# Where a decode layer's input x is loaded, and who copies its key tiles, in a kernel fed by one long stream of weights

## The chip, the cores and the metric

One core of a Trainium2 chip runs one launch. The metric is the device time in microseconds (us), here the median of three runs.

## The reference

One token goes through a transformer layer whose attention and gated feed-forward stand side by side on the same normalised input. All is float32.

```python
x  = A_x                                  # (1, 1, 1024)
xn = layernorm(x)                         # eps 1e-5, no weights
# attention: 32 query heads, 4 key heads, 128 wide; the last 4096 of 65536 cached positions
q = (xn @ wq)                             # wq 1024 x 4096
p = softmax(q k^T * 128**-0.5);  o = p v  # k, v: 4 x 4096 x 128
a = o @ wo                                # wo 4096 x 1024
# feed-forward
h = gelu(xn @ w_gate) * (xn @ w_up)       # 1024 x 3584 each
b = h @ w_down                            # 3584 x 1024
return x + a + b
```

Nearly all of the work is to read these weights and the window of the caches once: 94.38 MB by the profile.

## The kernel before

All large tensors pass through one tile in SBUF, `ring`, of 128 partitions x 32768 columns (16.8 MB). The list `PLAN` says in which order the loads are issued, to which column of the ring each goes, and which earlier load's data must have been used up before it may be issued. In order: `q` 0 and 1 (the halves of wq), `k` 0, `v` 0, `g` 0 (half of w_gate), `k` 1, `v` 1, `g` 1, `ua` 0, `ub` 0, `u` 1 (w_up), `o` 0 and 1 (wo), `m`, and `d` 0 to 2 (w_down). Every one of them is issued on SyncE's queue by `load`, so SyncE's queue is the order of the stream; a load that has to wait for its part of the ring holds up those behind it. The entry `m` stands for `load_moved`: ten small loads (`moved`) of a part of w_down's last rows.

A recording layer (`Flow`) stands between the code and the engines. Each operation goes to its engine in the order in which the code calls it. From the places that operations read and write it works out which must wait for which, and gives each waiting instruction its semaphores. All operations thus carry one line, L225, in the profile.

The first transfers do not go through the ring. `x_rows`, x as 2 rows of 512, is what the layer norm reads. `x_out`, x spread over four of the 128 partitions, is added to the output at the very end (`downs`, the addition of `out_p` and `x_out`). Both are issued on ScalarE's queue at the program's start: two transfers for `x_rows`, one for each row, and two for `x_out`. GpSimd builds the identity matrix `ident` at the start, and VectorE fills and builds the other constants. `layer_norm` then transposes `x_rows` on TensorE (`xt_p`, in the tag `tp`) and leaves the normalised x in `xz`. `xz` is what every product with wq, w_gate and w_up needs. Such a product is split: even rows go to TensorE (`blocks`, tile `acc`), odd rows are scaled and summed on VectorE (`add_scaled`, tile `part`).

Each load of keys holds two of the four key heads. For each head `transpose_keys` makes eight tiles `kT`: TensorE transposes four 128x128 blocks into one of two PSUM buffers (tag `tp`), and then one engine copies that buffer to SBUF. The argument `vector` lists the tiles that VectorE copies; ScalarE copies the others. Because there are two buffers, TensorE's tile i+2 waits for the copy of tile i. `scores` multiplies the eight tiles by the queries and finds the maximum on VectorE (`reduce_max`, an addition of `away`, a second `reduce_max`, and `bias`); `exponentials` runs on ScalarE. For a pair of heads the code stands in this order:

```python
transpose_keys(2 * i, kn[:, :half], range(8), (1, 4, 6))
if i == 0:
    queries(q_sb)
s = scores(2 * i)
transpose_keys(2 * i + 1, kn[:, half:], range(4), ())
exponentials(2 * i, s)
transpose_keys(2 * i + 1, kn[:, half:], range(4, 8), (4, 5, 7))
s = scores(2 * i + 1)
```

When the second head's last transposition is done, the keys' part of the ring is free and the next load into it (`k` 1, later `ua` 0) may be issued.

Of the kernel before, what the change touches and what calls it, by code (L numbers as in the profile page):

```python
# [19 lines left out]
NJ = D // (NR * P)  # L20
# [13 lines left out]
ROW = (31, 32, 95, 96)  # L34
# [231 lines left out]
def decode_layer(nc, x, k_cache, v_cache, wq, wo, w_gate, w_up, w_down, out):  # L266
# [16 lines left out]
    def source(kind, i):  # L283
        if kind == "q":
            return fours(wq, i)
        if kind == "g":
            return fours(w_gate, i)
        if kind[0] == "u":
            return fours(w_up, i)[:, {"u": slice(NR), "ua": slice(2), "ub": slice(2, NR)}[kind]]
        if kind in "kv":  # L290
            cache = k_cache if kind == "k" else v_cache
            return windows(cache, i)
        if kind == "o":
            return grouped(wo, P * WIDE * i, WIDE)
        return grouped(w_down, P * sum(DOWN[:i]), DOWN[i])
# [4 lines left out]
    def load(key, at):  # L300
        kind, i = key
        if kind == "m":
            load_moved()
            return
        src = source(*key)
        if kind in "kv":

            loaded[key] = dst = ring[:, at:at + RING // 4]
            if kind == "v":
                nc.sync.dma_start(dst, src)  # L310
            else:
                for odd in range(2):
                    nc.sync.dma_start(dst[odd:P:2], src[:, odd])
            return
        rows, n = src.shape[1:]
        loaded[key] = ring[:, at:at + rows * n]
        dst = loaded[key].rearrange("p (t n) -> p t n", n=n)
        pieces = PIECES[i] if kind == "d" else (0, rows)
        if key == ("d", 2):
            end = 2 * n - MC  # L320
            nc.gpsimd.memset(loaded[key][:, end:2 * n], 0.0)
            both = src[:, 0:2].rearrange("p t n -> p (t n)")
            nc.sync.dma_start(loaded[key][0:P:2, :2 * n], both[0:P:2])
            nc.sync.dma_start(loaded[key][1:P:4, :2 * n], both[1:P:4])
            nc.sync.dma_start(loaded[key][3:P:4, :end], both[3:P:4, :end])
            pieces = pieces[1:]
        for t, end in zip(pieces, pieces[1:]):
            ends = (0, n // 2, 3 * n // 4, n) if key == ("d", 2) and end == rows else (0, n)
            for cols in (slice(*cut) for cut in zip(ends, ends[1:])):
                nc.sync.dma_start(dst[:, t:end, cols], src[:, t:end, cols])  # L330
# [4 lines left out]
    def load_moved():  # L335


        rest = w_down[DF - 4 * P:, D - MC:].rearrange("(r x) n -> x r n", x=16)[13]
        for s, a, first, count, step in MOVED:
            for j in range(step):  # L340
                to = 32 * a + j
                nc.sync.dma_start(
                    moved[to:to + 4 * (count // step):4, s], rest[first + j:first + count:step]
                )

    def used(key):

        for new, at, old in PLAN:
            if old == key:
                load(new, at)  # L350


    x_rows = work.tile([NJ, NR * P], F32, name="x_rows")
    x_in = x.rearrange("a b (j p) -> (a b j) p", j=NJ)
    for j in range(NJ):
        nc.scalar.dma_start(x_rows[j:j + 1, :], x_in[j:j + 1, :])
    x_out = work.tile([P, CO], F32, name="x_out")
    nc.vector.memset(x_out, 0.0)
    x_in = x.rearrange("a b (h c n) -> (a b c) h n", h=2, c=4)
    for c in (0, 2):  # L360
        nc.scalar.dma_start(
            x_out[ROW[c]:ROW[c] + 2, :].rearrange("c (h n) -> c h n", h=2), x_in[c:c + 2]
        )

    ident = consts.tile([P, P], F32, name="ident")
    nc.gpsimd.memset(ident, 0.0)
# [43 lines left out]
    def small(name):  # L410
        return psum.tile([P, NB], F32, name=name, tag="tp", bufs=2)
# [56 lines left out]
    def project(kind, jj, w, rows, count):  # L468
        n = count * NB
        for k, r in enumerate(rows):  # L470
            first = jj == 0 and r < 2
            if first and r == 0:
                acc[kind] = psum.tile([P, 2, NB], F32, name="acc_" + kind, tag="acc")
                part[kind] = work.tile([P, 8 * NB], F32, name="part", tag="part")
            wr = w[:, k * n:(k + 1) * n]
            if r % 2 == 0:
                blocks(kind, xz[:, r, jj, :], wr, count, first, False)
            else:
                add_scaled(part[kind][:, :n], wr, xz[:, r, jj, 0:1], first)

    def projected(kind, count):
        blocks(kind, unit, part[kind], count, False, True)

    def query_rows():
        q_sb = work.tile([P, 2, NB], F32, name="q_sb", tag="rows")
        nc.scalar.activation(q_sb, acc["q"], AF.Copy)
        return q_sb

    def queries(q_sb):
        q_p = psum.tile([P, 2, 4, 4], F32, name="q_p", tag="tp", bufs=2)  # L490
        for b in range(2):
            for hh in range(4):
                nc.tensor.matmul(
                    q_p[:, b, hh, :], q_sb[:, b, hh * P:(hh + 1) * P], ident[:, 0:P:32],
                    start=True, stop=True,
                )
            nc.vector.tensor_copy(
                qz[:, b, 0:16].rearrange("p (s t h) -> p s t h", s=2, t=2),
                q_p[:, b].rearrange("p h (s t) -> p s t h", s=2),
            )  # L500
# [10 lines left out]
    def transpose_keys(g, kn, steps, vector):  # L511
        if g not in keys:
            keys[g] = work.tile([P, 8, NB], F32, name="kT")
        for i in steps:
            t_p = small("kt_p")
            for jj in range(4):
                j = 4 * i + jj
                nc.tensor.transpose(t_p[:, jj * P:(jj + 1) * P], kn[:, j * DH:(j + 1) * DH], ident)
            if i in vector:
                nc.vector.tensor_copy(keys[g][:, i, :], t_p)  # L520
            else:
                nc.scalar.activation(keys[g][:, i, :], t_p, AF.Copy)
# [19 lines left out]
    def exponentials(g, s):  # L542
        p = work.tile([P, 2, NB], F32, name="p", bufs=2)
        for odd in range(2):
            nc.scalar.activation(
                p.rearrange("p b (n odd) -> p odd (b n)", odd=2)[:, odd], s[:, odd], AF.Exp,
                bias=bias[:, g, odd:odd + 1], scale=SCALE, accum_out=l[:, g, odd:odd + 1],
            )
        probs[g] = p
# [223 lines left out]
    half = RING // 8  # L773
    for key, _, _ in PLAN:
        kind, i = key
        if kind == "m":
            continue
        if kind == "q":
            project("q", i, loaded.pop(key), range(NR), 8)
        elif kind == "k":  # L780
            kn = loaded.pop(key)
            if i == 0:
                projected("q", 8)
                q_sb = query_rows()
            transpose_keys(2 * i, kn[:, :half], range(8), (1, 4, 6))
            if i == 0:
                queries(q_sb)

            s = scores(2 * i)
            transpose_keys(2 * i + 1, kn[:, half:], range(4), ())  # L790
            exponentials(2 * i, s)
            transpose_keys(2 * i + 1, kn[:, half:], range(4, 8), (4, 5, 7))
            s = scores(2 * i + 1)
        elif kind == "v":
            vn = loaded.pop(key)
            pT = transpose_probs(2 * i)
            exponentials(2 * i + 1, s)
            values(2 * i, pT, vn[:, :half])
            values(2 * i + 1, transpose_probs(2 * i + 1), vn[:, half:])
            if i == 1:  # L800
                maxima()
        elif kind == "g":
            project("g", i, loaded.pop(key), range(NR), NA)
            if i == 1:
                state = factors()
                projected("g", NA)
                gelu()
        elif kind in ("ua", "ub", "u"):
            taken = {"ua": (0, 1), "ub": (2, 3), "u": range(NR)}[kind]
            project("u", i, loaded.pop(key), taken, NA)  # L810
            if kind == "ua":
                normalizers(*state)
            elif kind == "ub":
                heads()
        elif kind == "o":
            if i == 0:
                projected("u", NA)
                gated()
            outputs(i)
            if i == 0:  # L820
                hidden()
        elif i == 2:
            downs()
        used(key)
# [26 lines left out]
```

## Time and profile before

| what | value |
|---|---|
| median of 3 runs (lowest, highest) | 226.16 us (226.12, 226.31) |
| the profiled execution | 226.15 us |
| its span, from first to last instruction | 224.8 us |
| TensorE, VectorE, ScalarE, GpSimd busy | 126.0, 112.1, 28.2, 2.8 us |
| read from HBM | 94.38 MB, 420 GB/s over the span |
| time of SyncE's queue's packets (q1), of 16 DMA engines' span | 97.8% |

The span is 1.35 us shorter than the execution's time. q1 is SyncE's queue, q10 ScalarE's; q8 and q14 fetch instructions and the like. Where a row gives start and length, both are microseconds, the start from the span's start.

### The profile page before, as it was taken

What the parts mean: (1) busy time and instruction counts of PE and PEld (TensorE: products, weight loads), DVE (VectorE), ACT (ScalarE), POOL (GpSimd) and SP (SyncE); (2) the same over time, 40 slices, a digit from 0 to 9 for tenths busy, and PEclk for the clock granted to TensorE, in tenths of its full rate; (3) what the DMA queues carried; (4) which work ended last, traced back from release to release, by engine and by line L of the source; (5) the groups of instructions that cost most, each with busy time, mean ns of one, the idle gap of its engine ahead of it and who ended that gap; (6) DMA issues with size and microseconds to landing.
All of it is one profiled execution on the core that took longest, in us unless ns stands there. A gap on an engine that the chain in (4) does not pass through costs nothing.

```text
span 224.8 us, 2511 instructions
## 1 busy us (share of the span) xinstructions
PE 126.0 (56%) x1107; PEld 65.6 (29%) x1107; DVE 112.1 (50%) x142; ACT 28.2 (13%) x54; POOL 2.8 (1%) x9
## 2 busy tenths in 40 slices
PE   0120910539899891999836751237308988900976
PEld 0010200104634731755601110001003887400442
DVE  7030920591333282336039489339708932992942
ACT  2030000002415600454400220000000000000000
POOL 3000000000000000000000000000000000010000
PEclk9999975596969999799988795557965855665699
DMA  9889889799997999999989999999989989999994
GB/s 374 374 385 548 373 373 560 338 408 464 439 490 338 429 443 452 391 488 408 472 355 449 434 449 429 490 399 420 469 385 455 467 385 461 434 397 394 426 407 172
DMA packets 3194, 94.53 MB, mean 421 GB/s; under 512 B 446, under 2 KB 718, under 8 KB 1040
## 3 DMA queue, kind: packets, MB, share of 16 engines
q1 hardware_dynamic: 3160, 94.38, 97.8%
q8 instruction: 8, 0.13, 0.2%
q14 instruction: 2, 0.02, 0.0%
q10 hardware_dynamic: 24, 0.01, 0.0%
HBM read 94.38 MB, written 0.00 MB: 420 GB/s over the span
## 4 chain that ended last, share of the span: by engine, by line
DMA 67%; DVE 20%; PE 10%; SPq 1%; ACT 1%; issue 1%; POOL 0%; DVEq 0%
DMA ring<-in_B_w_gate 26%; DMA ring<-in_A_wq 18%; DMA ring<-in_A_wo 13%; DVE part L225 13%; DMA ring<-in_B_w_down 10%; PE tp L225 6%; PE out L225 3%; DVE out_part L225 3%; DVE rows L225 2%; SPq L225 1%; PE acc L225 1%; DVE g_sb L225 1%; ACT kT L225 1%; DVE hz L225 1%; DVE kT L225 0%
## 5 line engine op out<-in xcount | busy, mean ns | idle before, releaser
L225 PE MATMUL acc<-ring,xz 128*32 128x512 f32 x176 | 32.2, 808 | 37.3 <-DMA ring<-in_A_wq 22.2
L225 DVE SCALAR_TENSOR_TENSOR part<-ring,xz,part 128x3584 f32<-128x3584 f32 (+1 forms) x9 | 37.2, 4129 | 22.0 <-DMA ring<-in_A_wq 12.5
L225 PE MATMUL tp<-ident,ring 128*128 128x128 f32 x128 | 21.0, 309 | 7.1 <-DMA ring<-in_A_k_cache 5.0
L225 PEld LDWEIGHTS acc<-ring,xz 128*32 128x32 f32 x176 | 7.2, 139 | 58.2 <-issue 26.7
L225 DVE SCALAR_TENSOR_TENSOR out_part<-ring,oz,out_part 128x1024 f32<-128x1024 f32 x16 | 20.6, 1285 | 0.6
L225 PEld LDWEIGHTS tp<-ident,ring 128*128 128x128 f32 x128 | 15.4, 154 | 16.7 <-DMA ring<-in_A_k_cache 5.9
L225 PE MATMUL out<-ring,hz 128*32 128x256 f32 x168 | 12.1, 438 | 13.5 <-DMA ring<-in_B_w_down 13.4
L225 DVE COPY kT<-tp 128x512 f32<-128x512 f32 x12 | 8.1, 690 | 19.1 <-PE tp L225 19.1
L225 PE MATMUL out<-ring,oz 128*32 128x256 f32 x120 | 12.0, 586 | 9.6 <-DMA ring<-in_A_wo 9.6
L225 ACT ACTIVATE kT<-tp 128x512 f32<-128x512 f32 x20 | 11.5, 596 | 26.6 <-PE tp L225 26.6
L225 PE MATMUL tp<-ident,kT 128*128 128x4 f32 (+4 forms) x64 | 13.4, 343 | 1.6 <-DVE hz L225 1.6
L225 PEld LDWEIGHTS tp<-ident,kT 128*128 128x128 f32 (+2 forms) x64 | 13.1, 294 | 2.2 <-DVE hz L225 1.8
L225 PE MATMUL acc<-part,units 128*32 128x512 f32 x44 | 8.1, 817 | 8.7 <-DVE part L225 8.7
L225 DVE TENSOR_SCALAR part<-ring,xz 128x3584 f32<-128x3584 f32 (+1 forms) x3 | 6.5, 2171 | 12.3 <-DMA ring<-in_A_wq 7.5
L225 PEld LDWEIGHTS out<-ring,hz 128*32 128x32 f32 x168 | 5.6, 125 | 20.0 <-DMA ring<-in_B_w_down 15.8
L225 PEld LDWEIGHTS out<-ring,oz 128*32 128x32 f32 x120 | 5.7, 166 | 16.0 <-DMA ring<-in_A_wo 10.6
L225 DVE SCALAR_TENSOR_TENSOR out_part<-ring,hz,out_part 128x1024 f32<-128x1024 f32 x6 | 7.7, 1285 | 4.9 <-DMA ring<-in_B_w_down 4.7
L225 PE MATMUL s<-kT,qz 128*32 128x512 f32 x64 | 9.3, 709 | 0.0
L225 DVE TENSOR_REDUCE m<-s 128x2 f32<-128x1024 f32 x4 | 4.9, 1225 | 7.7 <-PE s L225 7.7
L225 PE MATMUL o<-ring,pT 128*32 128x128 f32 x256 | 7.8, 274 | 1.0 <-ACT pT L225 1.0
L225 PEld LDWEIGHTS o<-ring,pT 128*32 128x32 f32 x256 | 6.7, 110 | 1.9 <-ACT pT L225 1.9
L225 PE MATMUL tp<-ident,x_rows 2*128 2x2 f32 x4 | 0.6, 253 | 10.4 <-DMA x_rows<-in_A_x 10.4
(96 smaller groups left out, 73.3 us busy)
## 6 DMA issues: line engine op xcount, KB each, us to landing
ring<-in_B_w_gate SPq DMA_DIRECT2D x2, 7168.0 KB, 29.5
ring<-in_A_k_cache SPq DMA_DIRECT2D x4, 2048.0 KB, 19.0
ring<-in_A_v_cache SPq DMA_DIRECT2D x2, 4096.0 KB, 26.1
ring<-in_B_w_up SPq DMA_DIRECT2D x2, 3584.0 KB, 22.3
ring<-in_B_w_up SPq DMA_DIRECT2D x1, 7168.0 KB, 25.8
ring<-in_B_w_down SPq DMA_DIRECT2D x2, 2048.0 KB, 20.7
ring<-in_B_w_down SPq DMA_DIRECT2D x2, 512.0 KB, 21.1
ring<-in_B_w_down SPq DMA_DIRECT2D x2, 256.0 KB, 21.2
```

What stands on the lines that cost most here:

```text
L225: return lambda *a, **k: self.flow.issue(self.engine, lambda: call(*a, **k))
```

## The change

Three edits. The two transfers for `x_rows` become one of 2x512, issued on GpSimd's queue, ahead of all that GpSimd does for `ident`. The two transfers for `x_out` move from ScalarE's queue at the start to SyncE's queue, behind the ten loads of `moved` and ahead of `d` 0. And the tiles 1 and 3 of each pair's second head are copied by VectorE and no longer by ScalarE.

```diff
         if kind == "m":
             load_moved()
+            load_out()
             return
...
     x_rows = work.tile([NJ, NR * P], F32, name="x_rows")
-    x_in = x.rearrange("a b (j p) -> (a b j) p", j=NJ)
-    for j in range(NJ):
-        nc.scalar.dma_start(x_rows[j:j + 1, :], x_in[j:j + 1, :])
+    nc.gpsimd.dma_start(x_rows, x.rearrange("a b (j p) -> (a b j) p", j=NJ))
     x_out = work.tile([P, CO], F32, name="x_out")
     nc.vector.memset(x_out, 0.0)
-    x_in = x.rearrange("a b (h c n) -> (a b c) h n", h=2, c=4)
-    for c in (0, 2):
-        nc.scalar.dma_start(
-            x_out[ROW[c]:ROW[c] + 2, :].rearrange("c (h n) -> c h n", h=2), x_in[c:c + 2]
-        )
+
+    def load_out():
+        x_in = x.rearrange("a b (h c n) -> (a b c) h n", h=2, c=4)
+        for c in (0, 2):
+            nc.sync.dma_start(
+                x_out[ROW[c]:ROW[c] + 2, :].rearrange("c (h n) -> c h n", h=2), x_in[c:c + 2]
+            )
...
-            transpose_keys(2 * i + 1, kn[:, half:], range(4), ())
+            transpose_keys(2 * i + 1, kn[:, half:], range(4), (1, 3))
```

ScalarE's queue at the program's start (`x_rows` and `x_out` are the two loads of x, `st` and `zero` belong to the layer norm), with what the change takes out:

```order
-L225 DMA x_rows<-in_A_x 1x512 x2
-L225 DMA x_out<-in_A_x 2x2x128 x2
 L225 ACT_TABLE_LOAD
 L225 ACTIVATE st<-st 128x1
```

All four of its first transfers are gone, and its first instruction is now the table load.

SyncE's queue behind the second half of wo (`moved` are the small loads, `ring` the weights, here `d` 0 and the two halves of `d` 1):

```order
 L225 DMA moved<-in_B_w_down 5x768
 L225 DMA moved<-in_B_w_down 3x768
+L225 DMA x_out<-in_A_x 2x2x128 x2
 L225 DMA ring<-in_B_w_down 128x16384
 L225 DMA ring<-in_B_w_down 128x4096 x2
```

Two issues more stand ahead of the first load of w_down.

VectorE in the first pair of heads (`m` and `bias` are the end of `scores` of the pair's first head, `kT` the copies for its second head, the second `m_0` its scores):

```order
 L225 TENSOR_REDUCE m<-m_0 128x1
 L225 SCALAR_TENSOR_TENSOR bias<-m,away 128x2
-L225 COPY kT<-tp 128x512 x3
+L225 COPY kT<-tp 128x512 x5
 L225 TENSOR_REDUCE m_0<-s 128x2
 L225 TENSOR_TENSOR m_0<-m_0,away 128x2
```

The two added copies stand behind the first head's maximum and `bias`, not beside them; the same happens in the second pair. TensorE's order is unchanged.

## The prediction

> **What bounds the kernel now.** I read the page's head and queues first, then the stretches by window, then the chain that ended last.
>
> ```profile
> span 224.8 us, 2511 instructions
> DMA  9889889799997999999989999999989989999994
> ...
> q1 hardware_dynamic: 3160, 94.38, 97.8%
> q8 instruction: 8, 0.13, 0.2%
> ...
> q10 hardware_dynamic: 24, 0.01, 0.0%
> ```
>
> The sixteen DMA engines are busy in nearly every slice, and SyncE's queue (q1) alone fills 97.8% of their span. The windows (length, then busy time of TensorE, its weight loads, VectorE, ScalarE, GpSimd, then clock, DMA share and GB/s) say the same of each stage:
>
> ```profile
> 2.00:42.00 40.00, 8.11 (x44) 3.23 (x48) 12.30 (x31) 2.97 (x4) 0.65 (x2) 0.87 0.95 411
> 42.00:80.00 38.00, 31.92 (x307) 17.19 (x310) 17.18 (x19) 11.84 (x23) 0.00 (x0) 0.87 1.01 434
> 80.00:116.00 36.00, 24.46 (x270) 14.98 (x264) 13.81 (x20) 10.81 (x22) 0.00 (x0) 0.95 1.00 428
> 116.00:169.00 53.00, 22.83 (x117) 5.33 (x117) 33.76 (x30) 2.54 (x5) 0.00 (x0) 0.70 1.01 437
> 169.00:220.00 51.00, 35.66 (x336) 23.86 (x336) 32.86 (x36) 0.00 (x0) 0.74 (x1) 0.64 0.98 422
> ```
>
> No compute engine fills its window; DMA does, in all five. The chain's pieces (start, length, what) show why:
>
> ```profile
> 0.73 0.42 SPq L225
> ...
> 1.21 40.66 DMA ring<-in_A_wq
> ...
> 51.00 28.54 DMA ring<-in_B_w_gate
> ...
> 200.11 21.38 DMA ring<-in_B_w_down
> ```
>
> A load issued at 51.00 lands at 79.54 because its bytes stand behind others. So an engine that finishes later costs nothing until it makes SyncE issue a load so late that the stream runs dry. The time is the stream's start, 94.38 MB at its rate, and a tail of some 3 us after the last landing at 221.49. I cost each edit against that.
>
> **x_rows on GpSimd.** The timeline of the start (start, length, engine, operation):
>
> ```profile
> 0.73 0.79 ACTq L225 DMA_DIRECT2D x_rows<-in_A_x  x2
> 0.73 0.20 POOL L225 MEMSET ident<- 128x128 f32 x1 [0.29 <-POOLq L839]
> 0.73 0.89 SPq L225 DMA_DIRECT2D ring<-in_A_wq  x2
> ...
> 1.56 0.57 ACTq L225 DMA_DIRECT2D x_out<-in_A_x  x2
> ...
> 5.34 0.22 DVE L225 TENSOR_SCALAR away<-away 128x1 f32<-128x1 f32 x2
> ...
> 10.36 0.61 PE L225 MATMUL tp<-ident,x_rows 2*128 2x2 f32 x4 [10.36 <-DMA x_rows<-in_A_x]
> ...
> 14.94 0.23 DVE L225 TENSOR_SCALAR xz<-xc,st 128x8 f32<-128x8 f32 x1
> ...
> 22.67 6.25 PE L225 MATMUL acc<-ring,xz 128*32 128x512 f32 x32 [9.16 <-DMA ring<-in_A_wq]
> ...
> 26.43 1.17 SPq L225 DMA_DIRECT2D ring<-in_A_k_cache  x2
> 29.53 0.57 SPq L225 DMA_DIRECT2D ring<-in_A_v_cache  x1
> ```
>
> x was issued at 0.73 and let TensorE start at 10.36, 9.6 us later, since it shares the DMA engines with wq. From there `xz` takes 15.17 - 10.36 = 4.8 us, and the product with wq's first half cannot start before its load is in at 22.67. So x may be 22.67 - 15.17 = 7.5 us late before anything moves. Beyond that, only the next load counts: `k` 0 is issued 26.43 - 22.67 = 3.8 us after that product's start, and must be in the queue before wq's second half lands at 41.87, less the 0.5 us that the first load took from issue to its first data (0.73 to 1.21). So x may land as late as 41.87 - 0.5 - 3.8 - 4.8 = 32.8 us, against 10.4 now.
>
> When will it land? The trace has no transfer from GpSimd. The early end is about now, at 8 to 11 us: I assume that one transfer waits once behind wq's packets where two wait twice, but starts somewhat later. For the late end I let GpSimd get nothing done until VectorE has finished its constants (5.34 + 0.22 = 5.6 us) and then give x the 21.4 us of the last w_down load, the nearest row of a short load behind a full queue: 27 us. Even that is below 32.8. I take 12 us, nearer to the row of the same data, and a cost of 0. GpSimd's transfer also stands ahead of `ident`; `ident` is needed by VectorE's constants and by x's own transposition, and GpSimd could give it up to 9 us late before TensorE misses it.
>
> The Trainium skill speaks against this edit: its page "SBUF — State Buffer", section "SBUF: two separate sides", says that a transfer issued from GpSimd has its descriptors written by GpSimd's own cores, which a VectorE copy in a two-port mode locks out, and section "A bandwidth-pool intuition that's wrong (but worth ruling out)" names 620 ns that became some 3,100 in this way. By its figures x would land an estimated 2.5 us later, which the 7.5 us hold, so the sum stays; nothing before shows it.
>
> **The start of the stream.** With ScalarE's four transfers gone, SyncE's first load no longer shares the start.
>
> ```profile
> 51.00 0.33 SPq L225 DMA_DIRECT2D ring<-in_B_w_gate  x1
> ```
>
> Its issue took 0.42 us in the chain; this load alone took 0.33. The difference, 0.1 us, is what I take as gained. The ends are 0 and the 0.48 us between issue at 0.73 and first data at 1.21, since nothing can start before its issue. Everything behind is moved by as much.
>
> **x_out on SyncE.** Two issues more, ahead of `d` 0:
>
> ```profile
> 158.27 7.14 SPq L225 DMA_DIRECT2D moved<-in_B_w_down  x10
> ...
> 180.81 21.30 SPq L225 DMA_DIRECT2D ring<-in_B_w_down  x10
> ...
> 222.24 0.42 DVE L225 TENSOR_TENSOR y<-out,x_out 128x256 f32<-128x256 f32 x1 [6.12 <-PE out L225]
> ```
>
> The ten small loads end at 165.4. Two more at 0.7 us each end at 166.8, and `d` 0 is held until 180.81 by its part of the ring. So 14 us cover the 1.4 us. Without that cover it would cost 1.4. The reader of `x_out` is at 222.24; with the same 21.4 us to land it would be there at 188. The bytes through the engines are the same 4 KB as before. Cost 0.
>
> **Two more copies on VectorE.** The second head of the first pair, and what follows it:
>
> ```profile
> 65.81 1.23 DVE L225 TENSOR_REDUCE m<-s 128x2 f32<-128x1024 f32 x1 [3.36 <-PE s L225]
> 66.35 1.08 ACT L225 ACTIVATE kT<-tp 128x512 f32<-128x512 f32 x2 [5.99 <-PE tp L225]
> ...
> 67.45 0.16 DVE L225 SCALAR_TENSOR_TENSOR bias<-m,away 128x2 f32<-128x2 f32 x1
> ...
> 69.04 1.29 DVE L225 COPY kT<-tp 128x512 f32<-128x512 f32 x2 [1.43 <-PE tp L225]
> ...
> 71.07 1.12 SPq L225 DMA_DIRECT2D ring<-in_A_k_cache  x2
> ...
> 77.70 1.95 PE L225 MATMUL o<-ring,pT 128*32 128x128 f32 x64 [0.25 <-ACT pT L225]
> ...
> 79.56 2.08 DVE L225 TENSOR_SCALAR part<-ring,xz 128x3584 f32<-128x3584 f32 x1 [4.80 <-DMA ring<-in_B_w_gate]
> ...
> 81.16 3.17 PE L225 MATMUL acc<-ring,xz 128*32 128x512 f32 x23 [0.53 <-issue]
> ...
> 81.68 3.95 DVE L225 SCALAR_TENSOR_TENSOR part<-ring,xz,part 128x3584 f32<-128x3584 f32 x1
> ...
> 101.35 23.05 SPq L225 DMA_DIRECT2D ring<-in_B_w_up  x3
> ```
>
> ScalarE now copies tiles 0 and 1 from 66.35 to 67.43. On VectorE tile 1 has to wait behind the maximum and `bias`, until 67.61, and then takes 1.29 / 2 = 0.65 us: done at 68.3, 0.9 late. Tile 3 needs tile 1's buffer, and VectorE then copies tiles 3, 4 and 5 in a row, the fifth ending at about 71.0 where it ends at 70.33 now. So each pair gets about 0.7 us slower, not faster; between -0.3 (if alternation spares TensorE waits) and 0.9. In the first pair `k` 1 would be issued at 71.8, with `g` 0 still arriving until 79.54: nearly 8 us of cover. TensorE would end its heads at 80.35 instead of 79.65, with w_gate in at 79.56, so its product ends at 85.0 instead of 84.33; VectorE's half ends at 85.63 and frees the ring, as now. In the second pair `ua` 0 would be issued at 102.1. The load it follows, `g` 1, is far longer on its way:
>
> ```profile
> 111.42 0.38 PE L225 MATMUL tp<-ident,m 128*2 128x128 f32 x2
> ...
> 116.11 7.94 DVE L225 SCALAR_TENSOR_TENSOR part<-ring,xz,part 128x3584 f32<-128x3584 f32 x2 [3.48 <-DMA ring<-in_B_w_gate]
> ```
>
> It is in at 116.1: 14 us of cover, and TensorE, done at 111.8, has 4.3 us. Cost 0; with the cover gone it would be 2 x 0.7 = 1.4 us.
>
> **Sum.** 226.15 us (the profiled execution, 0.01 under the median) - 0.1 + 0 + 0 + 0 = 226.05, so 226.1.
>
> **Rivals.**
>
> *Slower: the new queue disturbs the stream at its start.* In the profile's list of queues q8's 8 packets take 0.2% of the span of all engines, 0.002 x 224.8 = about 0.45 us of stream, so a few interrupting packets can cost that much; the first 40 us run at 411 GB/s where the next 38 run at 434, so 40 x 23 / 434 = 2.1 us are lost there already. The price is between 0.45 and 2.1; I take 0.7, near the row of small packets: 226.8. It decides as soon as the wq halves land later than 22.67 and 41.87. Against it: x has only 4 KB. The Trainium skill's page "DMA: Bandwidth & Descriptors", section "Why a DMA increments its semaphore by 16 and not by 1", has a transfer from GpSimd post its completion from all 16 engines, one from ScalarE only from those it uses; that is a way for x to touch all of them. Chance 0.17.
>
> *Slower: x is late.* Past 32.8 us each microsecond of x costs one. Landing at 34 gives 227.3. Nothing in the trace speaks for it but that no GpSimd transfer is there. Chance 0.04.
>
> *Slower: a third queue costs time outside the span.* 226.15 - 224.8 = 1.35 us lie outside now; another queue to be started or closed may cost up to as much again. I take 1.0: 227.1. Chance 0.09.
>
> *Faster: x's loads on ScalarE cost the start more than I took.* The 2.1 us above may partly be theirs, and the first load may start up to 0.48 us earlier: 225.6 with half a microsecond. Against it: q10's 24 packets have 0.0% of the span. Chance 0.2.
>
> *No change*, as summed: 226.1, its own range 225.75 to 226.55. Chance 0.5.
>
> **The numbers.** A measurement of this kernel can tell about 0.2%, 0.45 us, from no change. No change has 0.5, faster by more than that 0.2, slower 0.17 + 0.04 + 0.09 = 0.3. The range reaches from 225.5 (most of the faster case) to 227.3 (all but the upper ends of the slower ones).
>
> **What would show it.** Right: x's transposition starts between 8 and 20 us; wq's first product still at 22.5 to 22.7; key loads issued about 0.7 us later than 71.07 and 101.35 with w_gate landing where it did; the last landing within 0.4 us of 221.49. Wrong: a window whose DMA share falls under 0.95 after 42 us; wq landing later; a larger gap between span and time; or the final addition waiting for `x_out`.

## The result: 0.5 us slower, at the program's end and outside the span

| | before | after |
|---|---|---|
| median of 12 runs (lowest, highest) | 226.16 us (226.03, 226.31) | 226.69 us (226.51, 226.85) |
| median span (before: of the 92 runs timed beside the experiments) | 224.8 us | 225.0 us |
| time outside the span (run's time minus its span), median (before: of the same 92) | 1.36 us | 1.69 us |
| ScalarE, VectorE, TensorE busy in the profile | 28.2, 112.1, 126.0 us | 26.0, 114.7, 122.7 us |

The ratio is 1.0022, with an interval of 1.0013 to 1.0031: slower, by about the 0.2% that the prediction took as what a measurement of this kernel can tell. The forecast was 226.1 us and no change. The profiled execution of the changed kernel took 226.85 us with a span of 225.2. The loss has two parts. Some 0.2 us are inside the span, and 0.33 us are outside it, where no instruction of the program lies.

The page of the changed kernel, its head and queues:

```profile
span 225.2 us, 2510 instructions
...
PE 122.7 (54%) x1107; PEld 65.1 (29%) x1107; DVE 114.7 (51%) x146; ACT 26.0 (12%) x50; POOL 3.5 (2%) x10
...
q1 hardware_dynamic: 3172, 94.38, 97.6%
...
q0 software_dynamic: 32, 0.00, 0.0%
...
q10 hardware_dynamic: 8, 0.00, 0.0%
```

The new queue q0 carries x, and q10, ScalarE's, is left with the 8 packets of the two output stores. The windows of the stream (columns as in the prediction):

```profile
42.00:80.00 38.00, 30.72 (x304) 16.67 (x304) 18.06 (x20) 10.65 (x21) 0.00 (x0) 0.88 1.00 430
80.00:116.00 36.00, 25.23 (x270) 15.98 (x270) 15.54 (x22) 9.84 (x20) 0.00 (x0) 0.90 1.00 431
116.00:169.00 53.00, 21.85 (x117) 5.09 (x117) 33.76 (x30) 2.54 (x5) 0.00 (x0) 0.73 1.02 438
169.00:220.00 51.00, 34.09 (x331) 23.25 (x335) 32.87 (x36) 0.00 (x0) 0.74 (x1) 0.65 0.98 421
```

The DMA share is as before in every one, between 0.98 and 1.02: the stream never ran dry. In the chain the stream's pieces end where they did, within a few tenths:

```profile
1.21 40.91 DMA ring<-in_A_wq
...
51.24 28.92 DMA ring<-in_B_w_gate
...
199.84 21.87 DMA ring<-in_B_w_down
```

The last landing is at 221.71, 0.22 us later than before, and wq had already come 0.25 us later. The first load varies by as much whatever the edit: in the thirteen profiles wq's first product starts between 22.59 (e1, e4) and 23.00 us (e7), and at 22.92 in e2, where `x_rows` is loaded as before. What is left is the end of the program. The timeline of the four output stores, first before, then after:

```profile
223.08 0.28 SPq L225 DMA_DIRECT2D out_y<-y  x1
223.09 0.27 ACTq L225 DMA_DIRECT2D out_y<-y  x1
223.40 0.28 ACTq L225 DMA_DIRECT2D out_y<-y_last  x1
223.63 0.26 SPq L225 DMA_DIRECT2D out_y<-y_last  x1
```

```profile
223.30 0.29 SPq L225 DMA_DIRECT2D out_y<-y  x1
223.31 0.52 ACTq L225 DMA_DIRECT2D out_y<-y  x1
...
223.84 0.27 SPq L225 DMA_DIRECT2D out_y<-y_last  x1
223.87 0.24 ACTq L225 DMA_DIRECT2D out_y<-y_last  x1
```

The first store on ScalarE's queue takes 0.52 us to issue where it took 0.27, and its second begins only at 223.87. ScalarE ends its issues at 224.11, level with SyncE; before, it was done at 223.68, 0.21 us ahead of SyncE (223.63 + 0.26). That matters for what follows: at the end of `finish` ScalarE counts a semaphore up behind its last issue (L202), and SyncE waits for it, clears the semaphores (L204) and waits for the last store to land (L206). SyncE's waits at the end (engine and line, what it waited for, us in total, times, longest), first before, then after:

```profile
SPq L206 <- SPq L206: 0.7, 1, 0.7
```

```profile
SPq L206 <- SPq L206: 0.9, 1, 0.9
SPq L204 <- ACTq L202: 0.2, 1, 0.2
```

The new row for L202 is not where the time goes. The clear at L204 starts at 224.18 and takes 0.10 us, so it is over 0.85 us before the wait at L206 ends at 225.14. What ends the span in both kernels is the landing of the last store, for which L206 waits. By the DMA packets in the trace SyncE's second store used to leave last (at 224.37, ScalarE's at 224.16). Now ScalarE's leaves last (at 224.61, SyncE's at 224.58), and the last landing comes 1.02 us after the end of SyncE's last issue, where it came 0.84 us after it before. That it is ScalarE's store that lands last is inferred from this order; the trace doesn't name the landings.

From the first store's start to the end of the span it now takes 225.2 - 223.30 = 1.9 us, and took 224.8 - 223.08 = 1.7 before. So of the 0.4 us between the two profiled spans about half is the later last landing and half is this.

### The profile page after: what moved, and what is told of

It is laid out like the page before. It is cut to its first block, busy times and chain, and to the rows that moved or that the text cites. A ratio compares the mean times of both kernels' runs of the same rounds, so it can differ in the third digit from the quotient of the medians.

```text
span 225.2 us, 2510 instructions
## 1 busy us (share of the span) xinstructions
PE 122.7 (54%) x1107; PEld 65.1 (29%) x1107; DVE 114.7 (51%) x146; ACT 26.0 (12%) x50; POOL 3.5 (2%) x10
## 4 chain that ended last, share of the span: by engine, by line
DMA 67%; DVE 19%; PE 10%; SPq 1%; ACT 1%; issue 1%; POOL 0%; DVEq 0%
DMA ring<-in_B_w_gate 26%; DMA ring<-in_A_wq 18%; DMA ring<-in_A_wo 13%; DVE part L225 13%; DMA ring<-in_B_w_down 10%; PE tp L225 6%; DVE out_part L225 3%; PE out L225 3%; DVE rows L225 2%; SPq L225 1%; PE acc L225 1%; DVE g_sb L225 1%; ACT kT L225 1%; DVE hz L225 1%; DVE kT L225 0%
## 5 line engine op out<-in xcount | busy, mean ns | idle before, releaser
L225 DVE COPY kT<-tp 128x512 f32<-128x512 f32 x16 | 10.9, 689 | 19.0 <-PE tp L225 19.0
L225 PE MATMUL out<-ring,hz 128*32 128x256 f32 x168 | 11.6, 424 | 14.8 <-DMA ring<-in_B_w_down 14.8
L225 PE MATMUL out<-ring,oz 128*32 128x256 f32 x120 | 11.3, 554 | 9.5 <-DMA ring<-in_A_wo 9.5
L225 ACT ACTIVATE kT<-tp 128x512 f32<-128x512 f32 x16 | 9.4, 596 | 29.2 <-PE tp L225 29.2
L225 PE MATMUL acc<-part,units 128*32 128x512 f32 x44 | 7.3, 754 | 8.4 <-DVE part L225 8.4
L225 PE MATMUL s<-kT,qz 128*32 128x512 f32 x64 | 7.7, 598 | 0.0
```

What stands on the lines that cost most here:

```text
L225: return lambda *a, **k: self.flow.issue(self.engine, lambda: call(*a, **k))
```

## The experiments

Each was timed in five rounds against the kernel before on the same chip; ratios are to it, with a 95% interval. e9, e10 and e11 were timed on another chip than the other eight; the kernel before took 226.20 us there, and 226.12 to 226.13 beside the others. "Fewer" counts how many instructions (copies and DMA issues together) ScalarE's program has less than in the kernel before. The changed kernel has 8 fewer: four copies and four DMA issues.

### One edit alone: e1_xrows_gpsimd, e2_xout_sync, e3_copies

```diff
# e1: before, and only this
-    for j in range(NJ):
-        nc.scalar.dma_start(x_rows[j:j + 1, :], x_in[j:j + 1, :])
+    nc.gpsimd.dma_start(x_rows, x.rearrange("a b (j p) -> (a b j) p", j=NJ))
# e2: before, and only this, in load_out behind load_moved
-        nc.scalar.dma_start(x_out[...], x_in[c:c + 2])
+        nc.sync.dma_start(x_out[...], x_in[c:c + 2])
# e3: before, and only this
-            transpose_keys(2 * i + 1, kn[:, half:], range(4), ())
+            transpose_keys(2 * i + 1, kn[:, half:], range(4), (1, 3))
```

> The kernel before with one edit: x_rows comes in one transfer on GpSimd's queue; x_out stays on ScalarE's queue at the start, key copies as before. Theory A (the loss is made of a later start of the stream, of ScalarE's first transfer of all now falling on the final store, and of time outside the span): the stream and the part outside the span carry what GpSimd's queue does, the final store does not, because ScalarE's queue has been used at the start. Time 226.16 + 0.0 to 0.3; ScalarE's two final stores 0.27 us each as in the kernel before. Rival B (GpSimd's transfer alone makes the loss): the whole 0.53, so 226.7. Rival C (the key copies make it): 226.16.

> The kernel before with one edit: x_out on SyncE's queue behind the small loads; x_rows stays in two transfers on ScalarE's queue at the start. Theory A: ScalarE's queue is used at the start by x_rows, so its final stores stay at 0.27 us each; nothing else lies on the path: 226.16, within 0.1. Rival B (two issues more on SyncE, or x_out's packets among the weights, cost the stream something): 226.3 to 226.7 with w_down's last landing later.

> The kernel before with one edit: VectorE copies tiles 1 and 3 of each pair's second head. Theory A: the stream covers it: 226.16, within 0.1. Rival C (the key stages cost through the stream or the clock): 226.4 to 226.7.

Measured: 226.21 us, 1.0003 [0.9994, 1.0012]; 226.23 us, 1.0003 [0.9994, 1.0012]; 226.24 us, 1.0007 [0.9998, 1.0016]. No edit costs anything that can be told by itself, and the upper ends of the three intervals (0.27, 0.27 and 0.36 us) are below the 0.53 us of the loss. Both e1 and e2 keep the 1.35 us outside the span, so neither a GpSimd queue nor two more issues on SyncE's is the cause by itself. These times alone don't exclude that three small costs add up; the experiments below show what the edits do together. In e3 the time outside was between 1.33 and 1.67 us from run to run, the first sign that something outside the span depends on the two programs that e3 changes, ScalarE's and VectorE's.

### Without the copies, and with ScalarE's queue used earlier: e5_both_moves, e4_warm_act

```diff
# e5: after, without the copies
-            transpose_keys(2 * i + 1, kn[:, half:], range(4), (1, 3))
+            transpose_keys(2 * i + 1, kn[:, half:], range(4), ())
# e4: after, with x_out issued at the same place by ScalarE
-            nc.sync.dma_start(
+            nc.scalar.dma_start(
                 x_out[ROW[c]:ROW[c] + 2, :].rearrange("c (h n) -> c h n", h=2), x_in[c:c + 2]
             )
```

> The changed kernel without the two more copies on VectorE: x_rows on GpSimd's queue and x_out on SyncE's, so ScalarE's first transfer of all is a final store. Theory A (each move is free, but together they leave ScalarE's queue unused until the final stores, whose first then takes 0.52 us): the whole loss is there, 226.6 to 226.7, with a first store of ScalarE at 0.52 us. Rival D (the time outside the span, 1.69 us in every execution of the changed kernel against 1.35 before, hangs on the lengths of the engines' programs, which the copies change too): the first store takes 0.52, but the part outside the span goes back to 1.35 and the time is 226.3.

> The changed kernel with one difference: x_out is loaded on ScalarE's queue instead of SyncE's, at the same place in the program (about 133 us), so ScalarE's queue has had a transfer before its final stores. Theory A: the first of ScalarE's final stores is issued in 0.27 us again instead of 0.52, and 0.25 us of the loss goes: 226.45. Rival B (the loss lies in GpSimd's transfer or in the start): unchanged at 226.7.

Measured: e5 226.56 us, 1.0017 [1.0008, 1.0027]; e4 226.16 us, 1.0000 [0.9992, 1.0009]. Moving both loads of x away from ScalarE brings most of the loss; leaving `x_out` there, 130 us into the program, brings all of it back. Theory A had expected less of e4, 226.45 us: it counted the long issue alone, and the time outside the span came back to 1.36 us with it. e5 lies between its two forecasts: the first store took 0.53 us, and the time outside was 1.46 to 1.66 us, neither 1.69 nor 1.35. The tile view of `x_out` in e4, and of `x_rows` in the kernel before (shortest, median and longest issue in ns, then the first and the last start):

```profile
L225 ACTq DMA_DIRECT2D x_out<-in_A_x x2: 256/404/553, 131.4 to 132.0; - x2
```

```profile
L225 ACTq DMA_DIRECT2D x_rows<-in_A_x x2: 230/378/526, 0.7 to 1.3; - x2
```

Of two equal issues one takes twice as long. The timelines show the same extra quarter microsecond for whichever transfer is the first of the program on ScalarE's queue: at 0.73 before, at 131.4 in e4, at the first output store after. With the first use behind it, e4's end is that of the kernel before: ScalarE's issues are done at 223.68, ahead of SyncE's:

```profile
223.09 0.29 SPq L225 DMA_DIRECT2D out_y<-y  x1
223.09 0.27 ACTq L225 DMA_DIRECT2D out_y<-y  x1
223.40 0.28 ACTq L225 DMA_DIRECT2D out_y<-y_last  x1
223.60 0.26 SPq L225 DMA_DIRECT2D out_y<-y_last  x1
```

### The first use taken out in two other ways: e8_warm_load, e7_stores_sync

```diff
# e8: after, one more transfer of 8 numbers behind x_out's
+        nc.scalar.dma_start(x_out[0:1, 0:8], x.rearrange("a b n -> (a b) n")[:, 0:8])
# e7: after, with all four output stores on SyncE
-        queue = nc.sync if (c > 0) == (h > 0) else nc.scalar
+        queue = nc.sync
```

> The changed kernel with one more load of 32 bytes of x, issued on ScalarE's queue before its final stores at about 133 us into a row of x_out that is never stored; x_out itself stays on SyncE's queue. Theory A: that load takes 0.5 us where nobody waits, ScalarE's first final store is back at 0.27, the part outside the span at 1.35: 226.16. Rival D or any cost of x_out on SyncE beside GpSimd's x_rows: 226.5 to 226.7.

> The changed kernel with all four final stores on SyncE's queue, so ScalarE's queue is never used. Theory A: the first store on a queue that has been used takes 0.28 us; four in a row on SyncE end later by 0.3 us than two on each queue, so the span grows by about 0.2, but what the first use costs is gone, with the part outside the span back at 1.35: 226.4 to 226.5. Rival D: the part outside stays at 1.69, 226.9.

Measured: e8 226.28 us, 1.0005 [0.9996, 1.0014], a mean span of 224.79 and 1.50 us outside; e7 226.49 us, 1.0017 [1.0008, 1.0026], a mean span of 225.20 and 1.34 us outside. In e8 the span is back at that of the kernel before (224.81), as the first use would have it, and still 0.14 us more than before stay outside. So a used queue alone doesn't explain the time outside. In e7 the four issues stand in a row on SyncE, and the end of the span is later for it:

```profile
223.42 0.60 SPq L225 DMA_DIRECT2D out_y<-y  x2
224.06 0.54 SPq L225 DMA_DIRECT2D out_y<-y_last  x2
```

They end at 224.60, 1.18 us after the first began, where two queues took 0.81; the time outside is 1.34 us with 10 fewer instructions.

### The length of ScalarE's program: e6_act_longer, e9_act_plus2, e11_act_plus1, e10_warm_short

In e6, e9 and e11 ScalarE computes a one-column exponential of a constant, which the kernel does once in the layer norm, nine, three and two times. The work is done long before `wq` is in. In e10 the used queue of e4 stays, and one copy more of each pair's first head goes to VectorE, so that ScalarE has again 8 fewer.

```diff
# e6 (e9: 3, e11: 2): after, with
-        zero = work.tile([P, 1], F32, name="zero")
-        nc.scalar.activation(zero, unit[:, 1:2], AF.Exp)
+        zero = work.tile([P, 9], F32, name="zero")
+        for i in range(9):
+            nc.scalar.activation(zero[:, i:i + 1], unit[:, 1:2], AF.Exp)
# e10: e4, with
-            transpose_keys(2 * i, kn[:, :half], range(8), (1, 4, 6))
+            transpose_keys(2 * i, kn[:, :half], range(8), (1, 3, 4, 6))
```

> The changed kernel with eight more tiny activations on ScalarE, in the layer norm, where ScalarE is idle (they write spare columns that nobody reads), so its program is as long again as in the kernel before. ScalarE's queue is still first used by the final stores. Theory A: no difference, 226.7, 1.69 us outside the span. Rival D (program length): 1.35 us outside the span, 226.35.

> The changed kernel with two more tiny activations on ScalarE in the layer norm (spare columns, read by nobody): ScalarE's program is then 6 instructions shorter than in the kernel before, not 8, as in the kernel with x_out on ScalarE's queue, but ScalarE's queue is still first used by the final stores. Theory A+D (two separate costs: the queue's first use in the span, about 0.15 us, and the length of ScalarE's program outside the span, 0.34 at 8 fewer, 0 at 6 fewer): 1.35 us outside, span 224.95, 226.3. Theory A alone (all of it is the queue): 226.69. Rival E (the part outside hangs on SyncE's two more instructions or on GpSimd's queue): 1.69 outside, 226.65.

> The changed kernel with one more tiny activation on ScalarE: 7 instructions fewer than before, as in the kernel with the 32-byte load, which had 1.50 us outside the span. Theory A+D: 1.50 outside, span 224.95, 226.45. Theory A alone: 226.69. Rival E: 1.69 outside.

> The kernel with x_out on ScalarE's queue (226.16, 1.35 outside the span), with one more tile of each pair's first head (tile 3) copied by VectorE instead of ScalarE: ScalarE's queue is used long before the final stores, but its program is 8 instructions shorter than in the kernel before, as in the changed kernel; SyncE's program is as in the kernel before. Theory A+D: span 224.8, 1.69 outside, 226.5. Theory A alone, or rival E: 226.16 with 1.35 outside. If the copies cost the stream anything, the span grows.

Measured: e6 226.28 us, 1.0010 [1.0001, 1.0019]; e9 226.30 us, 1.0008 [0.9999, 1.0017]; e11 226.48 us, 1.0014 [1.0005, 1.0023]; e10 226.52 us, 1.0016 [1.0007, 1.0025]. e9, e11 and e10 came out as the theory of two separate costs forecast; in e6 the part outside the span was that of rival D, and the long first store stayed.

All runs together, by what ScalarE's queue had done before its output store, and by the length of its program:

| kernel | used before? | fewer | median time | mean span | outside (lowest to highest) |
|---|---|---|---|---|---|
| before | yes | 0 | 226.16 | 224.81 | 1.31 to 1.43 |
| e1 | yes | 2 | 226.21 | 224.84 | 1.31 to 1.42 |
| e2 | yes | 2 | 226.23 | 224.87 | 1.32 to 1.38 |
| e3 | yes | 4 | 226.24 | 224.78 | 1.33 to 1.67 |
| e4 | yes | 6 | 226.16 | 224.81 | 1.32 to 1.43 |
| e8 | yes | 7 | 226.28 | 224.79 | 1.46 to 1.54 |
| e10 | yes | 8 | 226.52 | 224.84 | 1.66 to 1.77 |
| e6 | no | 0 | 226.28 | 224.98 | 1.30 to 1.42 |
| e5 | no | 4 | 226.56 | 224.95 | 1.46 to 1.66 |
| e9 | no | 6 | 226.30 | 224.98 | 1.30 to 1.40 |
| e11 | no | 7 | 226.48 | 224.98 | 1.47 to 1.57 |
| after | no | 8 | 226.69 | 224.99 | 1.64 to 1.75 |
| e7 | never used | 10 | 226.49 | 225.20 | 1.31 to 1.39 |

Two columns answer two questions. The mean span follows the queue: 224.78 to 224.87 where ScalarE's queue was in use before, 224.95 to 224.99 where the output store is its first transfer, whatever the length. The profiles say the same without the scatter of the weights' arrival: from the start of the first output store to the end of the span these five (e5, e6, e9, e11, after) take 1.83 to 1.85 us, and the seven with a used queue 1.66 to 1.71 us. The time outside follows the length: with 6, 7 and 8 fewer instructions it is 1.36, 1.50 and 1.70 us (medians of e4, e8, e10) with a used queue, and 1.36, 1.53 and 1.69 (e9, e11, after) without. One tiny activation more brings 0.16 us back, two bring all 0.33 back, and so do e6's eight. Meanwhile ScalarE's first store still takes its long issue, as the timeline of e9 shows:

```profile
222.99 0.29 SPq L225 DMA_DIRECT2D out_y<-y  x1
222.99 0.53 ACTq L225 DMA_DIRECT2D out_y<-y  x1
223.50 0.26 SPq L225 DMA_DIRECT2D out_y<-y_last  x1
223.57 0.25 ACTq L225 DMA_DIRECT2D out_y<-y_last  x1
```

So the two costs are separate, and each was taken away without the other. It isn't that a shorter program is worse: at 4 fewer the time outside varies from run to run, at 6 it is that of the kernel before, at 8 it is worst, at 10 (with ScalarE's stores gone too) it is good again.

What happens there is in the traces only in part; three of their records bear on it. One instruction packet of 8 KB (q14) comes at the program's end, later the shorter ScalarE's program is: within 0.1 us of the span's end with 0 fewer (before, e6), 0.3 us behind it with 2 fewer (e1, e2), 1.34 us behind it with 4 fewer (e3, e5), and it is not recorded with 6 or more. e6 and the changed kernel differ in ScalarE's added activations alone, so the packet hangs on ScalarE's program. With 7 fewer (e8, e11) the last but one update of semaphore 2 behind the span comes 0.16 to 0.18 us after the one before it, and in all other profiles 0.03 to 0.04 us after it: there the added time lies behind the span. With 8 fewer (e10, after) these updates end 1.46 us behind the span, no later than the 1.49 us of the kernel before, and the 1.7 us reach beyond them. An instruction fetch of ScalarE that falls into the program's last steps at some lengths and not at others would fit, but at 7 and 8 fewer, where the time is lost, no such packet is recorded. It stays open. No run varied another engine's length by itself.

No version beats both kernels: the best of them, e4, equals the one before.

## Why the prediction was wrong, step by step

**What bounds the kernel: right.** The stream of weights sets the time. From wq's landing (1.21 + 40.91 = 42.12) to the last landing at 221.71 the changed kernel took 179.59 us; before, from 41.87 to 221.49, 179.62. None of the edits inside it cost anything.

**x_rows on GpSimd: right in its sum.** The timeline of the changed kernel's start:

```profile
1.24 0.64 POOL L225 DMA_DIRECT2D x_rows<-in_A_x  x1 [0.79 <-POOLq L840]
...
10.83 0.61 PE L225 MATMUL tp<-ident,x_rows 2*128 2x2 f32 x4 [10.83 <-DMA x_rows<-in_A_x]
...
22.89 5.74 PE L225 MATMUL acc<-ring,xz 128*32 128x512 f32 x32 [8.91 <-DMA ring<-in_A_wq]
```

x is issued 0.51 us later and lands 0.47 us later than before, a little earlier than the 12 us that I took, and 7 us of cover remain. The Trainium skill's figure for descriptors that are locked out by VectorE (page "SBUF — State Buffer", section "A bandwidth-pool intuition that's wrong (but worth ruling out)") would have made it an estimated 2.5 us. This trace shows 0.47 us, no more than the later issue; but while the transfer was issued, from 1.24 to 1.88, VectorE ran only memsets, so the case of a VectorE copy beside it was not put to the test. The Trainium skill's page "DMA: Bandwidth & Descriptors", section "Why a DMA increments its semaphore by 16 and not by 1", has a transfer from GpSimd post its completion from all 16 DMA engines. q0's 32 packets for two rows fit that. e1, at 226.21 us, shows that they cost the stream nothing that can be measured. That ends the rival of the disturbed stream, and that of x too late with it.

**The start of the stream: the 0.1 us didn't appear.** wq's first product starts at 22.89, later than the 22.67 before and not earlier. In e1, where ScalarE's first transfers at the start are two of `x_out` in place of four, it starts earlier than in both:

```profile
22.59 5.36 PE L225 MATMUL acc<-ring,xz 128*32 128x512 f32 x32 [8.93 <-DMA ring<-in_A_wq]
```

One profile each can't tell such a difference from scatter, which is 0.4 us over all profiles: the mean spans of kernels with and without the early transfers (before 224.81, e4 224.81) show no gain. A term of 0.1 us was below what could be shown, and the prediction's sign for it, a first product at 22.5 to 22.7, failed, but the scatter is larger than what it was to show.

**x_out on SyncE: right.** Its issues lie in the gap ahead of `d` 0 as worked out, and `d` 0 was issued behind them at 181.05:

```profile
158.71 7.16 SPq L225 DMA_DIRECT2D moved<-in_B_w_down  x10
...
165.91 0.73 SPq L225 DMA_DIRECT2D x_out<-in_A_x  x2
...
181.05 20.79 SPq L225 DMA_DIRECT2D ring<-in_B_w_down  x10
...
222.46 0.42 DVE L225 TENSOR_TENSOR y<-out,x_out 128x256 f32<-128x256 f32 x1 [6.08 <-PE out L225]
```

Two issues took 0.73 us, half of the 1.4 that I took, and the final addition waits for TensorE, not for `x_out`.

**Two more copies on VectorE: right in direction and cost.** The second head of the first pair, after:

```profile
65.47 0.60 ACT L225 ACTIVATE kT<-tp 128x512 f32<-128x512 f32 x1 [4.57 <-PE tp L225]
...
66.56 0.16 DVE L225 SCALAR_TENSOR_TENSOR bias<-m,away 128x2 f32<-128x2 f32 x1
66.64 0.68 DVE L225 COPY kT<-tp 128x512 f32<-128x512 f32 x1
...
67.38 1.09 PE L225 MATMUL tp<-ident,ring 128*128 128x128 f32 x8 [0.59 <-DVE kT L225]
68.07 1.29 DVE L225 COPY kT<-tp 128x512 f32<-128x512 f32 x2 [0.75 <-PE tp L225]
...
70.95 1.12 SPq L225 DMA_DIRECT2D ring<-in_A_k_cache  x2
...
80.19 2.09 DVE L225 TENSOR_SCALAR part<-ring,xz 128x3584 f32<-128x3584 f32 x1 [5.54 <-DMA ring<-in_B_w_gate]
```

The first copy for VectorE stands behind `bias`, as worked out. From ScalarE's first copy to the load of `k` 1 it takes 70.95 - 65.47 = 5.48 us, and 71.07 - 66.35 = 4.72 before: 0.76 us slower, where 0.7 was forecast. Yet the load isn't issued 0.7 us later than 71.07, as I said it would be, since this stretch began 0.88 us earlier than before: in this execution TensorE had run the scores of the first head (16 products) in 1.92 us, and in 3.56 us before. Either way w_gate, in at 80.16, was what the engines waited for, and the 0.76 us cost nothing. In the second pair the same stretch takes 0.87 us more (from ScalarE's first copy at 99.25 to the load of `ua` 0 at 103.28, and from 98.19 to 101.35 before), and it also begins 1.06 us later, so `ua` 0 is issued 1.9 us later where 0.7 was forecast. `g` 1 is in at 116.36, which leaves 13 us of cover, so this cost nothing either.

**The failed step: what ScalarE's queue was left with.** Where the prediction counted "ScalarE's four transfers gone", it counted only a gain at the start. The "tail of some 3 us after the last landing" was taken as fixed (by the traces' spans it is 3.3 us before and 3.4 us after). There was no term for the queue's other transfers, the output stores, which became the first of the program and so took on the long first issue. In the kernel before, that lay in `x_rows` at 0.73 (0.79 us for two issues, where two for `x_out` took 0.57 us), where wq's load covered it; the change moved it to the one place that nothing covers. There the second store of ScalarE waits behind it, and the last store lands later. By the table's mean spans it costs 0.16 us: those of the five kernels whose output store comes first on the queue have a mean of 224.98, those of the seven with a used queue one of 224.82. The time from the first store's start to the span's end says the same, 1.84 us in the mean against 1.69.

**The second failed step: 1.35 us outside the span as a constant.** The sum started from the profiled execution's 226.15 us, and so held the 1.35 us outside the span fixed; only one rival let them change. That rival, a third queue, had the right place but the wrong cause and size: the queue on GpSimd costs nothing there (e1), while the shorter program of ScalarE costs 0.33 us (e10, with a used queue and 8 fewer instructions, has the same 1.70). The two make up the difference: 224.99 - 224.81 = 0.18 us of mean span and 1.69 - 1.36 = 0.33 us outside are 0.51 us, and 226.69 - 226.16 = 0.53 were measured. Among the prediction's signs of being wrong, the larger gap between span and time is the one that came.

**What was luck.** The 226.69 us lie inside the stated range and near the 226.8 of the rival of a disturbed stream. Neither speaks for the working: the stream was not disturbed, and none of the rivals had either of the two costs as its cause.

## What to carry to other kernels

When an edit empties an engine's DMA queue, look at what then becomes that queue's first transfer: if it is an output store at the end, leave one harmless earlier transfer on the queue, where something covers it. When a change of a few tenths of a percent can't be found in the span, subtract the span from each run's time before looking for it in the stages, and vary the number of instructions of an engine by one or two to see whether the difference hangs on that. Edits that cost nothing one at a time can cost together: each of the two moves here left the queue an earlier load, and only both left it none.

## What the runs showed of the hardware that was not expected

The first transfer that ScalarE issues in a program took 0.50 to 0.55 us to issue, and the later ones 0.22 to 0.28, whether the first came at 0.73, at 131 or at 223 us. SyncE's first load, at 0.73, doesn't tell the same so clearly: its 0.42 us in the chain stand against 0.33 for a later one.

The time between the span and the measured time, 1.31 to 1.43 us in all runs of the kernel before, rose to 1.7 us with eight instructions fewer on one engine, ScalarE, which was busy for 12% of the span, and one or two instructions of 0.2 us in an idle stretch took half or all of it back. In this kernel the length of one engine's program thus moved the time by 0.15%.
